# Gated attention and feed-forward kernel: fourth weight block split before the second up product, first low part of h before the softmax sums, output banks filled before the exponential

## The chip, the cores and the metric

The kernel runs on one core of one Trainium2 chip. A core has a matrix engine (TensorE, PE in the profile; PEld is its loading of weights), a vector engine (VectorE, DVE), an activation engine (ScalarE, ACT), a general engine (GpSimd, POOL) and an engine that here only issues transfers (SyncE, SP). ACT and POOL can issue transfers too; ACTq, SPq and POOLq are these issues. Each engine runs its own instructions in program order and waits on semaphores for the others. The metric is device time of one launch in microseconds (us); smaller is better.

## The reference

Everything is float32: 2048 tokens of width 512, 32 heads of 16, a window of 8 keys at distance 2, and a feed-forward part of width 1792 = 14 blocks of 128.

```python
xn  = layernorm(x)
qkv = xn @ wqkv                                    # q, k, v
logits[s, w] = q[s] . k[s - 2 w] / 4               # w = 0 .. 7, per head, masked where s - 2 w < 0
o   = softmax(logits) applied to v[s - 2 w]
s   = o @ wo
h   = relu(xn @ w1 + b1) ** 2
g   = silu(h @ w2 + b2)
out = x + s * g
```

## The kernel before

**Parts.** A float32 matrix product is made from two parts of each operand: a high part (ACT copies the value to the format that PE multiplies at full rate, `high`, line 119) and a low part (value minus high part, on DVE or POOL, `low`, line 122). Three products give the result: high times high, high times low, low times high (`PASSES`, line 25). `split` (line 125) makes both parts of one 128x512 tile. So before PE can use a block of weights, ACT and then POOL must have worked on it.

**Stages.** First come layer norm and the q, k, v products of the 16 token tiles; the last tiles save work with the scheme of `seven` (line 571), whose tiles are named X, Y, Z and U. Then come the four chunks `c` of 512 tokens (loop at line 895) with the feed-forward part. Attention itself runs on DVE beside all of it, as a stream of steps (`attention`, line 239): `qk` makes logits (tiles pr, L), `soft_a` subtracts the maximum (mx) and has ACT take the exponential, `soft_b` (line 288) makes the sums and their reciprocals (sm) on DVE and lets POOL scale L by them, `av` weighs the values (tiles pv, v), and `store_o` writes them out.

**Order by hand.** Every instruction keeps its program order on its engine. How many steps of the attention stream are put between two matrix products is decided by `pump(margin)` (line 366): it keeps an account of PE's and of DVE's time and emits steps while DVE's account stays below PE's plus the margin, in ns (`LATE` is 3000).

**Feed-forward blocks.** `up(c, f)` (line 672) makes block `f` of h for chunk `c`: 12 matmuls into a bank `ph`, then three instructions on ACT: Relu with bias in place, Square to the high part of `h`, Square in place (or into a tile `sq` for some blocks). `lowh(f)` (line 693) makes the low part of `h` on DVE (on POOL for the blocks with `sq`). The banks `ph` of two blocks alternate, so block f + 2 needs block f's bank read by `lowh(f)`. `down(pb, c, f, j)` (line 830) is three matmuls that add block `f`'s share of the output tile `j` to the bank `pb[j]`; PE makes `up(c, f)` and then the four `down` of block f - 2.

**Weight blocks.** The split weights of all 14 blocks stay in the core: `next_w` (line 391) splits the next block `f` (tiles named w: w1r, the block of w1, and w2r, the block of w2) and, from block 3 on, asks for the raw numbers of block f + 2 with `load_w` (line 382). The raw tiles are `piece`s of four buffers (line 116): block 5's raw numbers take the buffers of block 3's, and so can be asked for only when POOL has made block 3's low parts. Blocks 0 to 2 are split within the last stages of q, k, v; block 3 at the end of `seven` (line 661), block 4 ahead of `up(0, 2)`, and so on, one ahead of each `up` of chunk 0.

**The end of `seven`**, lines 653 to 663, for the last tiles: `next_w()` for block 2, `up(0, 0)`, the last product of Z, `pump(LATE)`, `up(0, 1)`, `next_w()` for block 3, `lowh(0)`, `pump(LATE)`.

**Turn from a chunk to the next**, lines 954 to 970: the last `down`, then `gate` for the four output tiles (in chunk 0 DVE adds b2 into tiles z, since the banks did not start from it; then ACT applies Silu to them), then `up(c + 1, 0)` and `up(c + 1, 1)` with a `pump` and `lowh` behind each, then the out product `pw` of an attention tile. The loop's next round starts with the four banks `pb`: from chunk 1 on ACT copies b2 into them (lines 896 to 899) and the matmuls of `down` add to that.

Of the kernel before, what the change touches and what calls it, by code (L numbers as in the profile page):

```python
# [26 lines left out]
TPC = C // P  # L27
# [30 lines left out]
def body(ctx: ExitStack, tc: tile.TileContext, x, wqkv, wo, w1, b1, w2, b2, out):  # L58
# [307 lines left out]
    def pump(margin=-SLACK):  # L366

        limit = clock["PE"] + margin
        flush(clock["PE"])
        while True:  # L370
            if coming[0] is None:
                coming[0] = next(stream, None)
            if coming[0] is None or clock["V"] + coming[0] > limit:
                break
            coming[0] = next(stream, None)
        if coming[0] is None:
            not_before(limit)
# [13 lines left out]
    def next_w():  # L391

        f = len(w12)
        if f < NF:
            w12[f] = buffer(f"w{f}", HOME[f]) if f in HOME else p2.tile([P, 2, 2, 512], FR, name=f"w{f}")
            for i, r in enumerate(raws.pop(f)):
                split(w12[f][:, 0, i], w12[f][:, 1, i], r, G)
            if 2 < f < NF - 2:
                load_w(f + 2)
# [171 lines left out]
    def seven(a):  # L571

        b = a + 1
        for s in (2, 0, 1):
            stgs[s] = pstg.tile([P, 4, 2, P], F32, name=f"stg{a}_{s}", tag="stg", bufs=5)
        sq_, sk_ = stgs[0], stgs[1]

        def x(t, h):
            return lambda p, k: xt[t][:, p, 2 * h + k]

        def s(i):
            return lambda p, k: ss[a][i // 2][:, i % 2, p, k]

        def product(ps, left, w, start=False, stop=False):
            n = 0
            for k in range(2):
                for p, r in PASSES:
                    PE.matmul(ps, left(p, k), w[:, r, k], start=start and n == 0, stop=stop and n == 5,
                              skip_group_check=True)
                    n += 1  # L590

        def groups(ps):
            return ps.rearrange("p (g c) -> p g c", g=4)

        more = a + 2 < NT
        X = psA(f"X{a}")
        product(X, x(a, 0), wq[0], start=True)
        Y = psH(f"Y{a}")
        A.activation(Y, X, AF.Copy)
        if a == SEVEN[0]:  # L600
            sum_high(a)
        first_norm(a)
        second_norm(a)
        pump(LATE)
        qkv(a, 2)
        if a > SEVEN[0]:
            sum_high(a)
        pump(LATE)
        while tail:
            tail.pop()()  # L610
        sum_low(a)
        if more:
            trans(a + 2)
        else:
            load_w(3)
        pump(LATE)
        qkv(b, 2)
        if more:
            trans(b + 2, True)
            lowx(a + 2)  # L620
        pump(LATE)
        product(X, x(a, 1), wq[1], stop=True)
        A.activation(sq_[:, :, 0], groups(X), AF.Copy, scale=0.25)
        pump(LATE)
        product(Y, s(1), tw[T2])
        Z = psH(f"Z{a}")
        A.activation(Z, Y, AF.Copy)
        if more:
            highx(b + 2)
        else:  # L630
            next_w()
        U = psA(f"U{a}")
        product(U, s(0), tw[T1], start=True, stop=True)
        A.activation(sk_[:, :, 0], groups(U), AF.Copy)
        if more:
            lowx(b + 2)
            sum_x(a + 2)
            next_stats(a)
        pump(LATE)
        product(Z, s(2), tw[T3])  # L640
        product(Y, s(3), wq[3], stop=True)
        pump(1500)
        V.tensor_add(sk_[:, :, 1], groups(Z), sk_[:, :, 0])
        V.tensor_add(sk_[:, :, 0], groups(Y), sk_[:, :, 0])
        store(a, 1, sk_)

        def last():
            product(Z, x(b, 1), tw[T4], stop=True)
            A.activation(sq_[:, :, 1], groups(Z), AF.Copy, scale=0.25)
            store(a, 0, sq_)  # L650

        tail.append(last)
        if not more:
            next_w()
            load_w(4)
            pump(LATE)
            up(0, 0, psT)
            tail.pop()()
            pump(LATE)
            up(0, 1, psT)  # L660
            next_w()
            lowh(0)
            pump(LATE)

# [227 lines left out]
    b2t = p2.tile([P, D], F32, name="b2t")  # L892
    dma(b2t, b2[None, :].to_broadcast([P, D]))

    for c in range(NCH):
        last = c == NCH - 1
        pb = [psA(f"pb{c}_{j}") for j in range(TPC)]
        if c:
            for j in range(TPC):
                A.activation(pb[j], b2t, AF.Copy)  # L900
        t0 = c * TPC
        room = ROOM if c else ROOM0
        for f in range(2, NF):
            if c == 0:
                next_w()
            up(c, f)
            pump()
            if c == 0 and f == 3:

                rwo = [p2.tile([P, 2, D], F32, name=f"rwo{i}", tag="oT", bufs=2) for i in range(2)]  # L910
                for i in range(2):
                    for q in range(4):
                        rows = wo[q * P + 64 * i:q * P + 64 * i + 64, :].rearrange("(g p) n -> p g n", g=2)
                        dma(rwo[i][32 * q:32 * q + 32], rows)
            if c == 0:
                if 6 <= f < 10:
                    split(wot[:, 0, f - 6], wot[:, 1, f - 6], rwo[(f - 6) // 2][:, (f - 6) % 2], G)
            elif f == 2:
                finish(t0 - 4)
            elif f == 3:  # L920
                finish(t0 - 3)
                trans_o(t0 - 2, psT(f"pT{t0 - 2}"))
                trans_o(t0 - 1, psT(f"pT{t0 - 1}"))
            elif f == 4:
                lowo(t0 - 2)
                lowo(t0 - 1)
            elif f == 5:
                out_product(t0 - 2, psT(f"pw{t0 - 2}"))
            elif f == 6:
                finish(t0 - 2)  # L930
                out_product(t0 - 1, psT(f"pw{t0 - 1}"))
            elif f == 7:
                finish(t0 - 1)
            if f == 2 and c:
                load_o(c * 2 - 1, True)
            elif f >= 7:
                load_o(c * 2, f >= 9)
            if f == 10:
                for i in range(2):
                    trans_o(t0 + i, psT(f"pT{t0 + i}"))  # L940
            if f == 11:
                for i in range(2):
                    lowo(t0 + i)
            if f >= 12:
                load_o(c * 2 + 1, last and f > 12)
            if not (last and f == NF - 1):
                for j in range(TPC):
                    down(pb, c, f - 2, j)
            pump(room)
            lowh(f)  # L950
        out_product(t0, psT(f"pw{t0}"))
        if last:
            out_product(t0 + 1, psT(f"pw{t0 + 1}"))
        pump(room)
        if not last:
            for i in range(2):
                for j in range(TPC):
                    down(pb, c, NF - 2 + i, j)
                if i == 0:
                    pump(room)  # L960
            pump()
            not_before(clock["PE"])
            for j in range(TPC):
                gate(c, j, pb)
            for i in range(2):
                up(c + 1, i)
                pump(ROOM)
                lowh(i)
            out_product(t0 + 1, psT(f"pw{t0 + 1}"))
            pump(ROOM)  # L970
        else:
            for i in range(2, TPC):
                trans_o(t0 + i, psH(f"pT{t0 + i}"))
            for i in range(2, TPC):
                lowo(t0 + i)
            xl = xTa.tile([P, TPC, 512], F32, name="xlast", tag="xT")
            dma(xl.rearrange("p (h e) n -> p h (e n)", e=2),
                x[t0 * P:(t0 + TPC) * P, :].rearrange("(h p e) n -> p h (e n)", p=P, e=2))
            for j in range(TPC):
                for f in range(NF - 3, NF):  # L980
                    down(pb, c, f, j)
                gate(c, j, pb)
                if j < 2:
                    finish(t0 + j, xl[:, j])
            for j in range(2, TPC):
                n = D // 2 if j == TPC - 1 else D
                for i in range(0, D, n):
                    cols = slice(i, i + n)
                    out_product(t0 + j, (psT if i else psH)(f"pw{t0 + j}_{i}"), cols)
                    finish(t0 + j, xl[:, j], cols)  # L990
# [21 lines left out]
```

## Time and profile before

| | us |
|---|---|
| median of 3 runs | 491.64 |
| these runs | 490.69 to 491.73 |
| the profiled execution, its own time | 489.87 |
| its span, first to last instruction | 487.9 |

The profile is of one execution. Its span leaves out 1.97 us that lie around the first and last instruction. All instructions that go through the helper that keeps the program order bear line 87, so rows are told apart by their tiles. A row of a timeline gives the start in the span, the length, the engine, the operation, what it writes and what it reads, how many it merges, and in brackets how long the engine sat idle before it and who released it. Matmuls overlap: a start-to-start distance of 2.72 us for 12 of them is what the timeline shows wherever nothing waits, while the row of 12 says 2.88 us, because the last of them is still draining. So PE's losses are read from distances between starts.

### The profile page before, as it was taken

What the parts mean: (1) busy time and instruction counts of PE and PEld (TensorE: products, weight loads), DVE (VectorE), ACT (ScalarE), POOL (GpSimd) and SP (SyncE); (2) the same over time, 40 slices, a digit from 0 to 9 for tenths busy, and PEclk for the clock granted to TensorE, in tenths of its full rate; (3) what the DMA queues carried; (4) which work ended last, traced back from release to release, by engine and by line L of the source; (5) the groups of instructions that cost most, each with busy time, mean ns of one, the idle gap of its engine ahead of it and who ended that gap; (6) DMA issues with size and microseconds to landing.
All of it is one profiled execution on the core that took longest, in us unless ns stands there. A gap on an engine that the chain in (4) does not pass through costs nothing.

```text
span 487.9 us, 5921 instructions
## 1 busy us (share of the span) xinstructions
PE 480.0 (98%) x2118; PEld 394.6 (81%) x2118; DVE 438.0 (90%) x374; ACT 227.8 (47%) x403; POOL 173.3 (36%) x153
## 2 busy tenths in 40 slices
PE   8999999999989999999999999999999999999996
PEld 6888888888768888887888888888888888888885
DVE  5997999999996999999999999999999979999243
ACT  5675667635455566327412434552242365223240
POOL 1325343655788998201233130412032014021100
PEclk9999999999999999999999999999999999999999
DMA  8799799994969682815362428255522745150231
GB/s 303 219 297 322 232 293 285 312 354 165 329 217 294 168 269 88 273 60 185 107 184 65 161 79 299 75 174 140 152 74 89 267 132 174 31 152 0 87 103 69
DMA packets 48520, 88.78 MB, mean 182 GB/s; under 512 B 5372, under 2 KB 32364, under 8 KB 45676
## 3 DMA queue, kind: packets, MB, share of 16 engines
q1 hardware_dynamic: 42444, 51.72, 33.9%
q10 hardware_dynamic: 4320, 33.56, 19.4%
q0 software_dynamic: 1728, 3.15, 3.9%
q8 instruction: 16, 0.26, 0.2%
q14 instruction: 12, 0.10, 0.1%
HBM read 57.94 MB, written 27.32 MB: 175 GB/s over the span
## 4 chain that ended last, share of the span: by engine, by line
PE 78%; DVE 9%; issue 6%; POOL 4%; ACT 2%; DMA 1%; ACTq 0%; DVEq 0%; POOLq 0%
PE pb L87 25%; PE ph L87 23%; PE pq L87 13%; PE pw L87 8%; PE X L87 3%; DVE L L87 3%; PE Z L87 3%; PE Y L87 3%; POOL w L87 2%; DVE v L87 2%; PE U L87 1%; DVE h L87 1%; DVE pr L87 1%; POOL ss L87 1%; DVE pv L87 1%
## 5 line engine op out<-in xcount | busy, mean ns | idle before, releaser
L87 PE MATMUL pb<-w,h 128*128 128x512 f32 x672 | 161.1, 389 | 1.2 <-ACT pb L87 0.8
L87 PEld LDWEIGHTS pb<-w,h 128*128 128x128 f32 x672 | 126.0, 188 | 28.2 <-ACT pb L87 1.2
L87 PE MATMUL ph<-xU,w 128*128 128x512 f32 x504 | 120.6, 389 | 0.0
L87 PEld LDWEIGHTS ph<-xU,w 128*128 128x128 f32 x504 | 94.6, 188 | 19.6
L87 ACT ACTIVATE ph<-ph,b1t 128x512 f32<-128x512 f32 x56 | 37.0, 660 | 150.6 <-PE ph L87 141.2
L87 DVE TENSOR_TENSOR pv<-v,L 128x2048 f32<-128x2048 f32 x32 | 78.4, 2449 | 1.3 <-POOL L L87 0.7
L87 DVE TENSOR_TENSOR pr<-k,q 128x2048 f32<-128x2048 f32 x32 | 75.8, 2368 | 0.5
L87 DVE TENSOR_REDUCE L<-pr 128x128 f32<-128x2048 f32 x32 | 73.0, 2280 | 0.4
L87 DVE TENSOR_REDUCE v<-pv 128x256 f32<-128x2048 f32 x32 | 72.7, 2273 | 0.4
L87 POOL TENSOR_TENSOR h<-sq,h 128x512 fp32r<-128x512 f32 x15 | 25.0, 1669 | 84.2 <-ACT sq L87 81.8
L87 DVE TENSOR_TENSOR h<-ph,h 128x512 fp32r<-128x512 f32 x41 | 27.8, 680 | 21.6 <-ACT ph L87 21.6
L87 PE MATMUL pw<-wot,oT 128*128 128x512 f32 (+1 forms) x204 | 46.0, 377 | 0.0
L87 PEld LDWEIGHTS pw<-wot,oT 128*128 128x128 f32 x204 | 36.8, 188 | 7.1
L87 PE MATMUL ph<-xT,w 128*128 128x512 f32 x168 | 40.5, 390 | 0.9 <-POOL w L87 0.9
L87 PEld LDWEIGHTS ph<-xT,w 128*128 128x128 f32 x168 | 31.5, 188 | 7.8 <-POOL w L87 1.3
L87 ACT ACTIVATE h<-ph 128x512 fp32r<-128x512 f32 x56 | 33.5, 599 | 2.6
L87 PE MATMUL pq<-wq,xt 128*128 128x512 f32 x144 | 34.4, 389 | 0.0
L87 POOL TENSOR_TENSOR L<-L,mx_None 128x512 f32<-128x512 f32 x7 | 17.6, 2515 | 41.6 <-DVE mx_None L87 41.6
L87 PEld LDWEIGHTS pq<-wq,xt 128*128 128x128 f32 x144 | 27.0, 188 | 5.6
L87 PE MATMUL pq<-wq,xT 128*128 128x512 f32 x132 | 30.8, 392 | 0.0
L87 PEld LDWEIGHTS pq<-wq,xT 128*128 128x128 f32 x132 | 24.5, 188 | 5.8 <-ACT xT L87 0.7
L87 POOL TENSOR_TENSOR L<-L,sm_None 128x512 f32<-128x512 f32 x7 | 11.4, 1622 | 47.3 <-DVE sm_None L87 47.3
(103 smaller groups left out, 552.7 us busy)
## 6 DMA issues: line engine op xcount, KB each, us to landing
k<-sk ACTq DMA_DIRECT2D x8, 1408.0 KB, 6.4
v<-sv ACTq DMA_DIRECT2D x8, 1408.0 KB, 9.0
sx<-xt SPq DMA_DIRECT2D x12, 512.0 KB, 4.9
xU<-sx ACTq DMA_DIRECT2D x6, 1024.0 KB, 8.9
x<-in_A_x SPq DMA_DIRECT2D x16, 256.0 KB, 5.7
sk<-stg SPq DMA_DIRECT2D x8, 512.0 KB, 4.4
sq<-stg SPq DMA_DIRECT2D x8, 512.0 KB, 4.6
sv<-stg SPq DMA_DIRECT2D x8, 512.0 KB, 5.7
```

The lines of the kernel that those rows point to most:

```text
L87: return tc.keep_in_program_order(f(*a, **k))
```

## The change

Three edits. First, `next_w()` for block 3 is called ahead of `up(0, 1)` and no longer behind it. Second, the `pump` in front of `up(0, 1)` has the margin 1500 in place of 3000, so that fewer steps of attention go ahead of `lowh(0)`. Third, the copies of b2 into the four banks of the next chunk are emitted right behind `up(c + 1, 1)`, ahead of the `pump` there, by a function that remembers the banks.

```diff
@@ -656,9 +656,9 @@
             pump(LATE)
             up(0, 0, psT)
             tail.pop()()
-            pump(LATE)
+            next_w()
+            pump(1500)
             up(0, 1, psT)
-            next_w()
             lowh(0)
             pump(LATE)
 
@@ -892,12 +892,19 @@
+    pbs = {}
+
+    def banks(c):
+        if c not in pbs:
+            pbs[c] = [psA(f"pb{c}_{j}") for j in range(TPC)]
+            if c:
+                for j in range(TPC):
+                    A.activation(pbs[c][j], b2t, AF.Copy)
+        return pbs[c]
+
     for c in range(NCH):
         last = c == NCH - 1
-        pb = [psA(f"pb{c}_{j}") for j in range(TPC)]
-        if c:
-            for j in range(TPC):
-                A.activation(pb[j], b2t, AF.Copy)
+        pb = banks(c)
         t0 = c * TPC
@@ -964,6 +971,8 @@
             for i in range(2):
                 up(c + 1, i)
+                if i == 1:
+                    banks(c + 1)
                 pump(ROOM)
                 lowh(i)
```

The program keeps every instruction it had. In the rows below the number behind a name is that of the buffer: w_1400 is block 2, w_1460 in the kernel before and w_1434 in the changed one are block 3, w_1485 is block 4, and a row that is there in both but under another number shows with - and +.

On POOL, at the start of chunk 0, the rows are the low parts of blocks 2, 3 and 4 and the scaling of L by its sums:

```order
 L87 TENSOR_TENSOR w_1400<-w1r_1155,w_1400 128x512
 L87 TENSOR_TENSOR w_1400<-w2r_1156,w_1400 128x512
+L87 TENSOR_TENSOR w_1434<-w1r_1326,w_1434 128x512
+L87 TENSOR_TENSOR w_1434<-w2r_1327,w_1434 128x512
 L87 TENSOR_TENSOR L_1106<-L_1106,sm_None 128x512
-L87 TENSOR_TENSOR w_1460<-w1r_1326,w_1460 128x512
-L87 TENSOR_TENSOR w_1460<-w2r_1327,w_1460 128x512
 L87 TENSOR_TENSOR w_1485<-w1r_1405,w_1485 128x512
 L87 TENSOR_TENSOR w_1485<-w2r_1406,w_1485 128x512
```

Block 3's two low parts now stand ahead of the scaling, which waits for DVE's reciprocal. On ACT, block 3's two high parts move likewise from behind the three instructions of `ph_1` to ahead of them.

On DVE, at the same place, the rows are the end of an `av` step, the low part of h for block 0, and the sums with their reciprocals:

```order
+L87 TENSOR_REDUCE v_499<-pv_3_1443 128x256
+L87 TENSOR_TENSOR h_0_1422<-ph_0_1409,h_0_1422 128x512
 L87 TENSOR_REDUCE sm_None<-L_1106 128x64
 L87 RECIPROCAL sm_None<-sm_None 128x64
-L87 TENSOR_TENSOR h_0_1422<-ph_0_1409,h_0_1422 128x512
```

The low part of block 0 moved from behind the sums to ahead of them; the row of v stands there in both kernels.

On ACT, at the turn from chunk 0 to chunk 1, the rows are the last instruction of `ph_1`, the four copies of b2, and the exponential of an attention unit (L_1901) with the load of the activation table for it:

```order
 L87 ACTIVATE sq_1_2114<-ph_1_2098 128x512
+L87 ACTIVATE pb_0_2116<-b2t 128x512
+L87 ACTIVATE pb_1_2117<-b2t 128x512
+L87 ACTIVATE pb_2_2118<-b2t 128x512
+L87 ACTIVATE pb_3_2119<-b2t 128x512
 L87 ACT_TABLE_LOAD
 L87 ACTIVATE L_1901<-L_1901 128x512
-L87 ACTIVATE pb_0_2134<-b2t 128x512
-L87 ACTIVATE pb_1_2135<-b2t 128x512
-L87 ACTIVATE pb_2_2136<-b2t 128x512
-L87 ACTIVATE pb_3_2137<-b2t 128x512
```

The copies moved ahead of the load and the exponential. At the two later turns they stood right behind `ph_1` already, and nothing moves there. Two small things move besides: about 25 us into chunk 0 one exponential and one split of `wo` trade places on ACT, and on SP one load of `wo` goes ahead of block 7's loads. PE's order is the same from beginning to end.

## The prediction

> **What bounds the kernel now.** The first page and the table of windows come first. A row of windows gives the stretch, its length, and the busy time and instructions of PE, PEld, DVE, ACT and POOL, then the granted clock, the transfers' share and their rate.
>
> ```profile
> span 487.9 us, 5921 instructions
> PE 480.0 (98%) x2118; PEld 394.6 (81%) x2118; DVE 438.0 (90%) x374; ACT 227.8 (47%) x403; POOL 173.3 (36%) x153
> ...
> 140.00:148.00 8.00, 6.70 (x28) 4.86 (x27) 7.93 (x8) 3.48 (x7) 6.99 (x5) 1.00 0.83 280
> 148.00:211.00 63.00, 63.00 (x280) 52.18 (x279) 58.93 (x39) 34.49 (x59) 46.33 (x25) 1.00 0.69 213
> 211.00:225.00 14.00, 13.21 (x59) 10.58 (x57) 13.73 (x11) 8.25 (x14) 2.38 (x2) 1.00 0.32 117
> 225.00:300.00 75.00, 74.98 (x331) 62.11 (x332) 73.74 (x52) 27.06 (x46) 19.03 (x11) 1.00 0.45 141
> ```
>
> PE is the bound: busy for 480.0 of 487.9 us at full clock (1.00), and what the kernel can win without less arithmetic is PE's idle time. Two of these stretches hold it: 140 to 148, the start of chunk 0, and the end of 211 to 225, the turn to chunk 1. Between them and behind them PE is busy throughout. The timeline of PE shows the places:
>
> ```profile
> 140.48 0.61 PE L87 MATMUL pb<-w,h 128*128 128x512 f32 x2
> 141.53 2.60 PE L87 MATMUL pb<-w,h 128*128 128x512 f32 x10 [0.43 <-DVE h L87]
> 143.97 0.62 PE L87 MATMUL ph<-xT,w 128*128 128x512 f32 x2
> 145.46 2.56 PE L87 MATMUL ph<-xT,w 128*128 128x512 f32 x10 [0.87 <-POOL w L87]
> 147.86 2.88 PE L87 MATMUL pb<-w,h 128*128 128x512 f32 x12
> ...
> 221.30 2.91 PE L87 MATMUL ph<-xU,w 128*128 128x512 f32 x12
> 225.02 3.01 PE L87 MATMUL pb<-w,h 128*128 128x512 f32 x12 [0.81 <-ACT pb L87]
> 227.87 2.88 PE L87 MATMUL ph<-xU,w 128*128 128x512 f32 x12
> ```
>
> The reader sees three waits: the low part of h for block 0 (DVE), the low part of weight block 3 (POOL), and the copy of b2 into the bank (ACT). They are the three edits' targets. The bracketed idle understates them, so I go by starts. From 140.48 to 147.86 PE makes 24 matmuls in 7.38 us; at 2.72 us for 12 these take 5.44, so the first two waits cost **1.94 us**. From 221.30 to 227.87 it makes 24 in 6.57 us, so the third costs **1.13 us**. All else that PE loses (the first 7 us, the drain at the end, some 0.1 to 0.2 us at the last products of Z) lies outside the change. The most that these edits can give directly is 1.94 + 1.13 = 3.07 us.
>
> **Edits one and two, the start of chunk 0.** The rows of POOL, ACT, DVE and SP at this place:
>
> ```profile
> 135.24 3.33 POOL L87 TENSOR_TENSOR w<-w2r,w 128x512 fp32r<-128x512 f32 x1
> 141.01 1.08 POOL L87 TENSOR_TENSOR L<-L,sm_None 128x512 f32<-128x512 f32 x1 [2.44 <-DVE sm_None L87]
> 142.05 3.35 POOL L87 TENSOR_TENSOR w<-w1r,w 128x512 fp32r<-128x512 f32 x1
> 145.36 1.29 POOL L87 TENSOR_TENSOR w<-w2r,w 128x512 fp32r<-128x512 f32 x1
> ...
> 137.96 0.66 ACT L87 ACTIVATE ph<-ph,b1t 128x512 f32<-128x512 f32 x1 [2.11 <-PE ph L87]
> 139.67 0.62 ACT L87 ACTIVATE w<-w1r 128x512 fp32r<-128x512 f32 x1
> 150.71 0.63 ACT L87 ACTIVATE w<-w1r 128x512 fp32r<-128x512 f32 x1 [7.20 <-DMA w1r<-in_B_w]
> 151.91 0.64 ACT L87 ACTIVATE ph<-ph,b1t 128x512 f32<-128x512 f32 x1
> ...
> 137.46 2.29 DVE L87 TENSOR_REDUCE v<-pv 128x256 f32<-128x2048 f32 x1
> 139.67 0.68 DVE L87 TENSOR_REDUCE sm_None<-L 128x64 f32<-128x512 f32 x1
> 140.85 1.22 DVE L87 TENSOR_TENSOR h<-ph,h 128x512 fp32r<-128x512 f32 x2
> 141.99 2.28 DVE L87 TENSOR_TENSOR pr<-k,q 128x2048 f32<-128x2048 f32 x1
> 153.70 0.69 DVE L87 TENSOR_TENSOR h<-ph,h 128x512 fp32r<-128x512 f32 x1 [3.66 <-ACT ph L87]
> ...
> 139.78 0.53 SPq L319 DMA_DIRECT2D so<-v  x1
> 140.40 0.54 SPq L549 DMA_DIRECT2D sq<-stg  x1
> 145.43 0.37 SPq L387 DMA_DIRECT2D w1r<-in_B_w  x1
> ```
>
> - *Low part of h, block 0.* It runs at 139.67 in the sums' place and is done by 139.67 + 0.68 = 140.35. PE needs it at its third matmul, 140.48 + 2 x 0.227 = 140.93. Covered by 0.6 us. The sums end 0.6 us later; only POOL's scaling waits for them.
> - *High parts of block 3 on ACT.* Two copies of at most 0.62 us each go from 139.67 into the 2.11 us in which ACT waited for PE ahead of 137.96. That idle time hides them; without it `ph_1` would be 1.24 us late. ACT waited for no transfer at 139.67, so the raw numbers are there.
> - *Low parts of block 3 on POOL.* POOL is free at 135.24 + 3.33 = 138.57, and was idle until 141.01 for the reciprocal. They now run from 138.57: one by 139.87, both by 141.15, at 1.29 us each (the row at 145.36). PE needs the first at 140.48 + 2.72 + 0.45 = 143.65. Covered by 3.8 us, even at the 3.35 us that such an operation takes beside DVE's large products (142.05).
> - *What follows on POOL.* The scaling starts at about 141.6 instead of 141.01, next to DVE's product at 141.99. Its cost there is between its 1.08 us and the 3.35 us of the row at 142.05. Then block 4's first low part, 1.29 to 3.35 us. With the long value for both it is done at 141.6 + 6.7 = 148.3; PE needs it in its next up product, at 148.64 + 0.45 = 149.1. I take the long value for the scaling and the short one for block 4: 146.3, nothing waits.
> - *Block 5's load.* Its transfer on SP stood at 145.43 because it waited for the low part of block 3 (ends 145.40). Now that wait ends at 139.87 and the order on SP decides: it follows the store of q, 140.40 + 0.54, so it is issued at about 141.0, 4.4 us earlier.
>
> ```profile
> DMA to landing us min/median/max: 2.9/4.9/5.6
> ```
>
> This is the answer on w1r's tile: from issue to landing at most 5.6 us. So the first half of block 5 is there by 146.6, the second by about 147.1. ACT then makes its two high parts and the three instructions of `ph_3` by about 149.5 instead of 153.67 (151.91 + 1.76). DVE, which waited 3.66 us for these, is ready at 150.04. So **DVE wins its 3.66 us**, with 0.5 us to spare on ACT's side; no PE wait hangs on it at this point, but the turn does.
>
> A rule of the Trainium skill speaks against this step: "DMA: Bandwidth & Descriptors", section "Queues, rings and completion order", says that each engine of the transfers goes round between the queues that have work, so the load of v (1408 KB on ACT's queue, issued at 142.94) would share the rate with block 5's. The load measured here shared with it as well, so the landing row already holds that; by the rule the spare half microsecond could go, not the 3.07.
>
> **Edit three, the turn.** The rows of DVE and ACT before PE's third wait:
>
> ```profile
> 215.50 2.48 DVE L87 TENSOR_TENSOR z<-pb,b2t 128x512 f32<-128x512 f32 x4
> ...
> 222.55 1.28 ACT L87 ACT_TABLE_LOAD   x1
> 224.38 2.14 ACT L87 ACTIVATE pb<-b2t 128x512 f32<-128x512 f32 x4
> ```
>
> ACT is a chain here: Silu behind DVE's additions, two blocks of h, the table load, the exponential, then the copies. PE started 225.02 - 224.38 = 0.64 us after the first copy did. With the copies ahead of the load the first starts at 222.55, 1.83 us earlier, and PE may start at 223.19. It would be there at 221.30 + 2.72 = 224.02, so on that clock the wait is gone with 0.8 us to spare, and the other three copies (2.14 / 4 = 0.54 us each) keep ahead of PE's three matmuls for a bank (0.68 us). But PE now comes 1.94 us earlier, at 222.08, and the copy comes earlier only by what DVE won, since ACT's chain hangs on the additions. With 3.66 us won, the additions start at about 211.84 (PE ended the banks three products ahead of 221.30, at 213.14, now 211.2), and the copies at 222.55 - 3.66 = 218.9, some 3 us before PE. DVE needs to win only 223.19 - 222.08 = 1.11 us for the wait to go whole.
>
> Given back: the exponential now comes behind 2.14 us of copies, but its reader, the sums, stands behind four `av` steps of DVE. The three instructions of `ph_2` behind it keep their place, since the same work precedes them. At the later turns nothing moves and PE waits for nothing. Behind 227.87 PE runs without a gap to the end in the kernel before, with DVE busy 73.74 of 75 us; DVE is moved up at least as far as PE (3.66 against 3.07 us), so no wait should form.
>
> **Sum.** 1.94 + 1.13 = 3.07 us. The profiled execution would take 489.87 - 3.07 = 486.8 us (span 484.8). Its time is 1.77 us below the median of the runs; carried to the median, 491.64 - 3.07 = **488.6 us**, 0.62% less.
>
> **Rivals.**
>
> *DVE becomes the bound of the turn.* If block 5's load lands no earlier than before, or the scaling stretches DVE's product and the wait at 153.70 stays, the additions still start at 215.50. Then PE may start on the banks at 223.19 and wins 225.02 - 223.19 = 1.83 us in all, whatever it won at 140: 489.8 us. For it: DVE has next to no idle time from 153.70 to 218. Against it: the load goes 4.4 us earlier, and a move of 1.11 us is enough.
>
> *The edits miss.* If the first low part stays late because the reduce at 137.46 moves, PE loses 141.53 - 140.93 = 0.60 us there again and the sum is 2.47, 489.2 us. If both new orders are taken up by waits right behind them (block 4 a microsecond or two late, then the turn on DVE's clock), the gain falls below 1 us: about 491 us, no change that can be told.
>
> *Slower: POOL held by DVE.* Block 4's low part now stands behind a scaling that begins just as DVE starts a large product. From 148.3 (two held operations) PE's need at 149.1 is 0.8 us away; each further held operation costs 3.35 us. It decides against the change once block 4 is done after 149.1 + 3.07 = 152.2. With two further holds it is done at 155.0, PE waits 5.9 us and loses 2.8 on balance: 494.5 us. For it: two of the three low parts of w in the rows above took over 3.3 us. Against it: never more than one operation was held per DVE product, and there is one product in this stretch.
>
> The Trainium skill's "GPSIMD Engine Reference", section "Specifications", says that GpSimd shares its SBUF interfaces with VectorE and contends with instructions that have two SBUF inputs. The trace agrees: 3.35 us beside the product of k and q at 141.99, 1.29 us at 145.36. By the rule block 3's low parts, now beside a reduce, stay short, and only the scaling is exposed, which is how it was priced above.
>
> **Chances and range.** The forecast 0.68; DVE at the turn or the first wait left (489.2 to 489.8) 0.17; no change that can be told 0.10; slower 0.05. The range reaches down to where runs scatter (the fastest run of before lies 0.95 below the median, the profiled one 1.77: 488.6 less 1.4 is 487.2) and up past the DVE rival with the same scatter of some 0.4 us, 490.2. About 0.2%, 1 us, is what a measurement here can tell from no change; the cases faster by more than that are the first two, 0.85; within it 0.10; slower 0.05.
>
> **What would show it.** Right: PE's starts from the pb row of block 0 on stand 2.72 us apart without a bracket; ACT's wait for w1r of block 5 shrinks from 7.20 us and ends by 147; DVE's 3.66 us before the low part of h is gone; the additions z start about 212; the first copy stands ahead of the table load, and PE's bracket with ACT pb is gone. Wrong: a bracket on PE naming POOL w one block later, DVE's wait for ACT ph still there, or new brackets on PE behind the turn, where there are none now.

## The result and the profile after

The changed kernel takes 488.07 us (median of 6 runs, 486.48 to 488.28) against 490.63 us for the kernel before, timed beside it (6 runs, 489.64 to 491.73). The ratio of the means, 487.70 to 490.75 us, is **0.9938**, with a 95% interval of 0.9917 to 0.9959: 3.04 us or 0.62% less. The forecast was 3.07 us, 0.62%. The medians lie only 2.56 us (0.52%) apart and the interval reaches from 0.41 to 0.83%, so it is luck that the two percentages agree to the digit. The forecast time of 488.6 us started from a median of 491.64 us for the kernel before, which beside the changed one stands at 490.63.

First come the page's head and the same windows as before (PE, PEld, DVE, ACT, POOL, clock, transfers' share and rate), of the changed kernel:

```profile
span 485.0 us, 5918 instructions
PE 478.9 (99%) x2118; PEld 394.4 (81%) x2118; DVE 439.8 (91%) x374; ACT 228.2 (47%) x403; POOL 173.7 (36%) x153
...
140.00:148.00 8.00, 8.00 (x37) 6.62 (x36) 7.93 (x8) 4.18 (x9) 7.49 (x5) 1.00 0.92 316
148.00:211.00 63.00, 63.00 (x279) 52.09 (x278) 62.55 (x40) 32.52 (x56) 43.69 (x24) 1.00 0.69 208
211.00:225.00 14.00, 13.96 (x63) 11.22 (x61) 13.76 (x12) 10.20 (x17) 2.38 (x2) 1.00 0.38 142
```

PE has no idle time left in the first stretch (6.70 of 8.00 us busy before) and next to none in the third (13.21 of 14.00 before). The span is 2.9 us shorter. In the second stretch it is DVE that changed: busy for 62.55 us where it was 58.93. The timeline of PE in the changed kernel, at the two places:

```profile
140.31 2.88 PE L87 MATMUL pb<-w,h 128*128 128x512 f32 x12
143.03 2.88 PE L87 MATMUL ph<-xT,w 128*128 128x512 f32 x12
145.75 2.88 PE L87 MATMUL pb<-w,h 128*128 128x512 f32 x12
...
216.51 2.88 PE L87 MATMUL pw<-wot,oT 128*128 128x512 f32 x12
219.43 3.02 PE L87 MATMUL ph<-xU,w 128*128 128x512 f32 x12
222.28 2.88 PE L87 MATMUL pb<-w,h 128*128 128x512 f32 x12
```

At the start of chunk 0 the 24 matmuls take 145.75 - 140.31 = 5.44 us: all 1.94 us are won. At the turn no bracket names ACT's copies any more, but two distances are still long: 219.43 - 216.51 = 2.92 and 222.28 - 219.43 = 2.85, where 2.72 is the rule. Together PE loses 0.33 us there, and of the 1.13 us 0.80 are won: 2.74 in all in this profile. (The span is shorter by 0.17 us more, because PE was that much earlier at the first row of pb.) The table of waits for the weight loads of PE between 210 and 230 us says what the remainder is (who waited, for whom, us in total, times, longest):

```profile
PEld ph L87 <- DVE h L87: 0.5, 1, 0.5
```

The third up product of chunk 1 needs the bank of the first, and that one is read by DVE's low part of h. In the kernel before this row of DVE was:

```profile
220.34 0.69 DVE L87 TENSOR_TENSOR h<-ph,h 128x512 fp32r<-128x512 f32 x1 [0.17 <-ACT ph L87]
```

It ended at 221.03, and PE began the third up product 0.27 us later, at 221.30. In the changed kernel it ends at 219.37 (row of 218.68 below), and PE begins 0.06 us later. So about 0.21 us were spare before, and since PE comes 1.94 us earlier to this point, DVE must win about 1.73 us if PE is not to wait here. The other engines at the start of chunk 0, in the changed kernel:

```profile
138.34 1.29 POOL L87 TENSOR_TENSOR w<-w1r,w 128x512 fp32r<-128x512 f32 x1
141.40 1.09 POOL L87 TENSOR_TENSOR L<-L,sm_None 128x512 f32<-128x512 f32 x1 [0.51 <-DVE sm_None L87]
142.45 3.34 POOL L87 TENSOR_TENSOR w<-w1r,w 128x512 fp32r<-128x512 f32 x1
153.21 1.29 POOL L87 TENSOR_TENSOR w<-w1r,w 128x512 fp32r<-128x512 f32 x1 [1.62 <-ACT w L87]
159.27 1.29 POOL L87 TENSOR_TENSOR w<-w2r,w 128x512 fp32r<-128x512 f32 x1
...
139.46 0.68 DVE L87 TENSOR_TENSOR h<-ph,h 128x512 fp32r<-128x512 f32 x1
141.78 2.85 DVE L87 TENSOR_TENSOR pr<-k,q 128x2048 f32<-128x2048 f32 x1
147.47 2.97 DVE L87 TENSOR_TENSOR pr<-k,q 128x2048 f32<-128x2048 f32 x1
153.27 3.37 DVE L87 TENSOR_TENSOR pr<-k,q 128x2048 f32<-128x2048 f32 x1
159.47 3.25 DVE L87 TENSOR_TENSOR pr<-k,q 128x2048 f32<-128x2048 f32 x1
213.84 2.48 DVE L87 TENSOR_TENSOR z<-pb,b2t 128x512 f32<-128x512 f32 x4
218.68 0.69 DVE L87 TENSOR_TENSOR h<-ph,h 128x512 fp32r<-128x512 f32 x1 [0.17 <-ACT ph L87]
...
146.04 0.63 ACT L87 ACTIVATE w<-w1r 128x512 fp32r<-128x512 f32 x1 [3.74 <-DMA w1r<-in_B_w]
152.50 0.63 ACT L87 ACTIVATE w<-w1r 128x512 fp32r<-128x512 f32 x1 [3.50 <-DMA w1r<-in_B_w]
220.46 2.17 ACT L87 ACTIVATE pb<-b2t 128x512 f32<-128x512 f32 x4
...
140.83 0.84 SPq L387 DMA_DIRECT2D w1r<-in_B_w  x1
145.81 0.38 SPq L387 DMA_DIRECT2D w1r<-in_B_w  x1
```

Block 3's low parts run from 138.34, the first low part of h at 139.46, block 5's load goes at 140.83 and is there at 146.04: each step within some 0.6 us of where the prediction put it. DVE's wait of 3.66 us is gone. But its additions z start at 213.84, not at 211.84. Set against the first row of pb, which the two profiles have at 140.48 and 140.31, they come 1.49 us earlier. DVE won less than half of what was forecast, and the question for the experiments was where the rest went and whether it matters.

### The profile page after: what moved, and what is told of

Read it like the earlier page. It is cut to its first block, busy times and chain, and to the rows that moved or that the text cites. A ratio compares the mean times of both kernels' runs of the same rounds, so it can differ in the third digit from the quotient of the medians.

```text
span 485.0 us, 5918 instructions
## 1 busy us (share of the span) xinstructions
PE 478.9 (99%) x2118; PEld 394.4 (81%) x2118; DVE 439.8 (91%) x374; ACT 228.2 (47%) x403; POOL 173.7 (36%) x153
## 4 chain that ended last, share of the span: by engine, by line
PE 98%; DMA 1%; DVE 0%; POOL 0%; issue 0%; ACT 0%; POOLq 0%
PE ph L87 31%; PE pb L87 31%; PE pq L87 14%; PE pw L87 9%; PE Z L87 3%; PE Y L87 3%; PE X L87 3%; PE U L87 2%; DMA x<-in_A_x 1%; PE pxT L87 0%; DVE z L87 0%; DVE st L87 0%; POOL rs L87 0%; DVE xn L87 0%; ACT scratch L87 0%
## 5 line engine op out<-in xcount | busy, mean ns | idle before, releaser
L87 DVE TENSOR_TENSOR pr<-k,q 128x2048 f32<-128x2048 f32 x32 | 78.3, 2447 | 0.6
```

The lines of the kernel that those rows point to most:

```text
L87: return tc.keep_in_program_order(f(*a, **k))
```

## The experiments

PE's loss below is the sum of its distances over 2.72 us for 12 matmuls, from the first row of pb on. DVE's gain is the start of the additions z minus the start of that row, against the kernel before (215.50 - 140.48 = 75.02 us).

| kernel | PE loses at the start | at the turn | elsewhere | DVE's gain | ratio of times, interval |
|---|---|---|---|---|---|
| before | 1.94 | 1.13 | 0 | 0 | 1 |
| changed, 1st profile | 0 | 0.33 | 0 | 1.49 | 0.9938, 0.9917 to 0.9959 |
| changed, 2nd | 0 | 0 | 0 | 2.47 | 0.9935, 0.9913 to 0.9958 |
| changed, 3rd | 0 | 0.34 | 0.09 | 1.45 | |
| edit one | 0.78 | 0 | 0 | 2.54 | 0.9959, 0.9945 to 0.9973 |
| edit two | 0 | 1.14 | 0 | 1.94 | 0.9972, 0.9957 to 0.9986 |
| edits one and two | 0 | 0.48 | 0 | 2.30 | 0.9945, 0.9933 to 0.9957 |
| edit three | 1.92 | 0.02 | 0 | -0.01 | 0.9981, 0.9970 to 0.9992 |
| low parts left out | 0 | 0 | 0 | 3.36 | |
| Silu later | 0 | 0.04 | 0.23 | 1.53 | 0.9940, 0.9918 to 0.9961 |
| more loads | 0 | 0.36 | 0.53 | 0.98 | |
| POOL held | 0 | 0.35 | 0.87 | 0.66 | |

The theory to test was the prediction's: three separate waits, and behind them DVE, which needs to win 1.11 us so that the turn does not take back what the start gave. Its rivals: DVE sets the turn, the waits hang on one edit, POOL becomes the bound.

**Edit one alone.**

```diff
             tail.pop()()
+            next_w()
             pump(LATE)
             up(0, 1, psT)
-            next_w()
             lowh(0)
```

> Edit one alone: block 3 is split ahead of the second up product, the margin stays 3000, the copies of b2 stay where they were. The low part of h for block 0 then stays behind the sums, so the theory of separate waits expects PE's wait on DVE h to stay (24 matmuls from the first pb row in 5.44 + 0.6 = 6.0 us, before 7.38) and its wait on POOL w to go: 1.3 us won at the start of chunk 0. At the turn the first copy still stands behind the table load and the exponential, and comes earlier only by what DVE wins (1.5 us by the changed kernel's trace): in all 1.3 to 1.5 us. If both waits hang on the one edit, all 1.94 us are won at the start.

PE's timeline of this kernel:

```profile
140.43 0.61 PE L87 MATMUL pb<-w,h 128*128 128x512 f32 x2
141.49 2.60 PE L87 MATMUL pb<-w,h 128*128 128x512 f32 x10 [0.44 <-DVE h L87]
143.92 2.89 PE L87 MATMUL ph<-xT,w 128*128 128x512 f32 x12
146.65 2.88 PE L87 MATMUL pb<-w,h 128*128 128x512 f32 x12
```

The wait on block 3 goes, the wait on the low part of h stays: 146.65 - 140.43 - 5.44 = 0.78 us. So the two waits are separate. The turn, though, lost nothing, without edit three: PE came 0.78 us later and DVE had won 2.54 us, more than expected, and the copies stood ready behind the exponential. In all 2.29 us, where 1.3 to 1.5 were expected.

**Edit two alone.**

```diff
             tail.pop()()
-            pump(LATE)
+            pump(1500)
             up(0, 1, psT)
             next_w()
```

> Edit two alone: the margin is 1500, block 3 is split behind the second up product as before. On DVE the low part of h goes ahead of the sums, and on POOL the scaling of L falls behind block 3's low parts too, since the step of attention is emitted later. ACT makes block 3's high parts at about 139.7 to 140.7, so POOL could make the first low part by about 141.6, ahead of PE's need at 143.6. If edit two carries the start by itself: 24 matmuls from the first pb row in 5.44 us, 1.94 us won, and edit one is worth only the earlier load of block 5 (issued at about 141.7 instead of 140.83). If edit one is needed for block 3: PE's wait on POOL w stays, and 0.6 us are won there.

POOL and PE of this kernel:

```profile
140.10 1.29 POOL L87 TENSOR_TENSOR w<-w1r,w 128x512 fp32r<-128x512 f32 x1 [1.80 <-ACT w L87]
...
140.22 2.88 PE L87 MATMUL pb<-w,h 128*128 128x512 f32 x12
142.94 2.88 PE L87 MATMUL ph<-xT,w 128*128 128x512 f32 x12
145.66 2.88 PE L87 MATMUL pb<-w,h 128*128 128x512 f32 x12
219.11 2.92 PE L87 MATMUL ph<-xU,w 128*128 128x512 f32 x12
222.83 3.02 PE L87 MATMUL pb<-w,h 128*128 128x512 f32 x12 [0.80 <-ACT pb L87]
```

Both waits at the start go by this edit alone. It puts the sums behind the low part of h on DVE, and with them POOL's scaling behind block 3; block 3's first low part waits for ACT until 140.10 and is still 2 us early. At the turn the old wait stands unchanged (1.14 us): PE comes 1.94 us earlier and DVE wins 1.94, so the copies move exactly as far as PE does. This is the mechanism of the rival in which DVE sets the turn: the copies hang on DVE's additions.

**Edits one and two, without three.** The two edits above together.

> Edits one and two, without three. As the prediction had it (DVE wins 3.66 us) the copies would be early enough behind the exponential too, and edit three worth nothing: 3.07 us won. By the changed kernel's trace, where DVE won 1.5 us, the first copy would start at 220.46 + 1.28 + 0.53 = 222.3 and PE on the banks 0.64 later, at 222.9, against 222.28 with edit three: PE's wait on ACT pb is back with 0.6 to 0.9 us, and about 2 us are won in all.

PE and DVE of this kernel:

```profile
219.37 2.88 PE L87 MATMUL ph<-xU,w 128*128 128x512 f32 x12
222.44 3.01 PE L87 MATMUL pb<-w,h 128*128 128x512 f32 x12 [0.19 <-ACT pb L87]
225.29 2.88 PE L87 MATMUL ph<-xU,w 128*128 128x512 f32 x12
...
156.88 0.69 DVE L87 TENSOR_TENSOR h<-ph,h 128x512 fp32r<-128x512 f32 x1 [1.12 <-ACT ph L87]
```

PE wins 2.59 us and waits for the copies again, 0.48 us with the restart. So without edit three 0.48 us are left at the turn, where a gain of 3.66 us on DVE would have left nothing; with edit two alone 1.14 are left, and with edit one alone, where PE comes later, nothing. What edit three has to win hangs on how far DVE gets ahead of PE. (Edit three beside only one of the others was not run.) PE wins a little more here than DVE's 2.30 us, because ACT also had 0.44 us of idle time ahead of its second block of h in the kernel before and has 0.15 now. By the times alone this kernel cannot be told from the changed one.

**Edit three alone.** The function `banks` and its call behind `up(c + 1, 1)`, with the old order at the end of `seven`.

> Edit three alone. The start of chunk 0 stays as in the kernel before (7.38 us for the 24 matmuls, both waits there). At the turn the copies stand ahead of the table load, 1.83 us earlier on ACT; PE is there 1.0 us earlier than now, so its wait on ACT pb goes whole: 1.1 us won. If the wait only changes its name (the bank of the next up product, the exponential's reader), less than 0.5 us is won.

PE's timeline at the turn:

```profile
221.79 2.90 PE L87 MATMUL ph<-xU,w 128*128 128x512 f32 x12
224.53 2.88 PE L87 MATMUL pb<-w,h 128*128 128x512 f32 x12
```

The start is as before (1.92 us lost), the turn loses 0.02 us: 1.11 us won, as expected. The wait on the copies changed to no other name.

**The changed kernel again**, beside two variants of it.

> The changed kernel again, beside the next two on the same chip: ratio 0.994, PE's starts as in its first profile (24 matmuls from the first pb row in 5.44 us; 0.2 us late at the third up product of chunk 1, whose bank waits for the low part of h of its first block).

Here PE's distances are 2.72 us throughout; the turn loses nothing and the whole 3.07 us are won. The third profile, below, lost 0.34 there. What differs is DVE. Its timeline in this second profile, with one row of POOL:

```profile
153.27 3.34 DVE L87 TENSOR_TENSOR pr<-k,q 128x2048 f32<-128x2048 f32 x1
159.44 2.29 DVE L87 TENSOR_TENSOR pr<-k,q 128x2048 f32<-128x2048 f32 x1
159.68 3.20 POOL L87 TENSOR_TENSOR w<-w2r,w 128x512 fp32r<-128x512 f32 x1 [0.31 <-ACT w L87]
212.82 2.47 DVE L87 TENSOR_TENSOR z<-pb,b2t 128x512 f32<-128x512 f32 x4
```

The product at 159.44 takes 2.29 us where the first profile had 3.25, and z starts 1.02 us earlier (212.82 against 213.84). POOL's row says why. In the first profile POOL's operation began at 159.27, 0.20 us ahead of the product, ended at 160.56, and the product ended 2.16 us behind that. In the second it began at 159.68, 0.24 us behind the product; the product kept its 2.29 us, and POOL's row grew to 3.20. So the one that starts first runs its length, and the other ends nearly as if it had begun when the first was done.

All profiles here bear this out (the one with POOL held is left aside, since its rows are merged). Of their 155 products of two tiles (pr and pv) between 130 and 215 us, the 62 that found no operation of POOL running took 2.28 to 2.29 us, and the 93 that found one ended 2.14 to 2.18 us behind its end.

> The changed kernel a third time, for its profile: PE's starts at the turn show whether the 0.33 us that the first profile lost there (none in the second) come and go with the start of DVE's additions z (213.84 in the first, 212.82 in the second). Expected: below 213.5 no loss, above it 0.1 to 0.4 us.

DVE in the third profile:

```profile
214.04 2.47 DVE L87 TENSOR_TENSOR z<-pb,b2t 128x512 f32<-128x512 f32 x4
```

Here z starts at 214.04, and the turn loses 0.34 us: the loss comes and goes with DVE, as expected. (Of the times, this run is a single one: 487.32 us.)

**Low parts of blocks 5 to 13 left out.** ACT writes zeros in their place, so POOL's subtraction is gone.

```diff
-                split(w12[f][:, 0, i], w12[f][:, 1, i], r, G)
+                if f < 5:
+                    split(w12[f][:, 0, i], w12[f][:, 1, i], r, G)
+                else:
+                    high(w12[f][:, 0, i], None, r)
+                    A.activation(w12[f][:, 1, i], r, AF.Copy, scale=0.0)
```

> The changed kernel with the low parts of the weight blocks 5 to 13 left out: ACT writes zeros in their place, POOL's subtraction is gone. If POOL's operations stretch DVE's large products (2.29 us alone, up to 3.37 in the changed kernel's rows between 148 and 193), the products fall to about 2.3 us except beside the low parts of wo and the scaling of L, DVE's additions z start 2 to 3 us earlier than 213.84, and PE's 0.2 us at the third up product of chunk 1 go. If ACT or the transfers set DVE's pace, the additions stay at about 213.8.

DVE of this kernel:

```profile
147.78 2.29 DVE L87 TENSOR_TENSOR pr<-k,q 128x2048 f32<-128x2048 f32 x1
153.13 2.29 DVE L87 TENSOR_TENSOR pr<-k,q 128x2048 f32<-128x2048 f32 x1
157.51 0.69 DVE L87 TENSOR_TENSOR h<-ph,h 128x512 fp32r<-128x512 f32 x1 [2.09 <-ACT ph L87]
212.24 2.47 DVE L87 TENSOR_TENSOR z<-pb,b2t 128x512 f32<-128x512 f32 x4
```

Without POOL's operations beside them the second, third and fourth product take 2.29 us each (the first, still beside block 4's low part, takes 2.85 as in the changed kernel), the gain on DVE is 3.36 us, and PE loses nothing. So POOL's operations do stretch them. About 1.5 of the 3.36 us come from four products between 171 and 195, which POOL stretched in the kernel before too, so the figure is not what the change by itself would win without the stretch. And a wait of 2.09 us stands behind the third product: DVE waits for ACT, which waits for the load of block 6 (and then, in this kernel, also writes the zeros). That is the second half of the answer: the wait of 3.66 us did not only go, part of it moved one block on.

**Silu behind the first up block of chunk 1**, meant to take the last 0.33 us.

```diff
-        A.activation(z, pb[j] if c else z, AF.Silu)
+        else:
+            A.activation(z, pb[j], AF.Silu)
...
                 up(c + 1, i)
+                if c == 0 and i == 0:
+                    for j in range(TPC):
+                        A.activation(gs[c, j], gs[c, j], AF.Silu)
```

> The changed kernel with chunk 0's four Silu moved behind ACT's three instructions of chunk 1's first up block. If the 0.33 us that PE still loses at the turn come from the low part of h waiting for ACT behind the Silu, DVE makes it without its 0.17 us of idle time, PE's distance of 2.92 us ahead of the third up product falls to 2.72 to 2.8, and the kernel wins 0.2 to 0.3 us more on PE's starts (too little for the times). If the late Silu holds ACT's next block, the copies of b2 come late instead and PE waits for ACT pb again, 0.3 us or more lost.

DVE's 0.17 us of idle time goes and the third up product starts on time (0.04 us lost at the turn), with DVE as late as in the first profile (1.53). But PE then loses 0.23 us two up products on, where its weight load waits for DVE's low part of h again. The loss moved; this is no better kernel.

**More loads ahead of block 6's.**

```diff
     dma(b2t, b2[None, :].to_broadcast([P, D]))
+    for n in range(2):
+        dma(p2.tile([P, D], F32, name=f"more{n}", tag=f"sq", bufs=2), w2[n * P:(n + 1) * P, :])
```

> The changed kernel with two further loads of 256 KB, which nothing reads, ahead of block 6's on SP. If DVE's gain is cut by block 6's load (ACT waited 3.5 us for it and DVE up to 2.1 us behind ACT), it lands some 1.5 us later than 152.5 (512 KB at the 340 GB/s of this stretch), DVE's wait behind the third product grows to 2 to 4 us, and the additions z start 1 to 2 us later than in the changed kernel, at 214 to 215; PE then loses at the turn (ph behind DVE h or pb behind ACT) 0.3 to 1.5 us. If products stretched by POOL are all that cuts it, z stays at 212.8 to 213.8 and PE as it was.

Block 6 is there at 153.38, 13.3 us behind the first row of pb, against 12.2 in the first and second profile of the changed kernel and 13.2 in the third: not clearly later, so the 512 KB did not do what they were meant to. DVE's gain is 0.98 us, less than in any of the three (1.45 to 2.47), z starts at 214.11, and PE loses 0.89 us in all, always for DVE's low part of h. But DVE's wait behind the third product is 1.36 us, not the 2 to 4 expected and no longer than the 1.52 of the third profile; the rest is in the five large products, which take 13.76 us: 3.66 - 1.27 - 1.36 = 1.03 of the measured 0.98. So this is no test of the load.

**POOL held.** Block 4's first low part is made three times.

```diff
                 split(w12[f][:, 0, i], w12[f][:, 1, i], r, G)
+                if f == 4 and i == 0:
+                    for n in range(2):
+                        low(w12[f][:, 0, i], w12[f][:, 1, i], r, G)
```

> The changed kernel with the first low part of block 4 made three times over on POOL (the same values). It ends at 145.8 now, and PE needs it at 149.1 by the prediction's sum. Two more operations of 1.3 to 3.3 us end it at 148.4 to 152.4; one of them falls beside DVE's product at 147.5, so about 150.4: PE waits about 1.3 us for POOL w in the up product of block 4, and the 24 matmuls from the pb row of block 1 take 6.7 instead of 5.44 us. If PE does not wait for POOL here, the slower rival's place was wrong.

POOL and PE of this kernel:

```profile
142.65 6.10 POOL L87 TENSOR_TENSOR w<-w1r,w 128x512 fp32r<-128x512 f32 x3
...
145.92 2.88 PE L87 MATMUL pb<-w,h 128*128 128x512 f32 x12
148.64 2.88 PE L87 MATMUL ph<-xT,w 128*128 128x512 f32 x12
151.36 2.88 PE L87 MATMUL pb<-w,h 128*128 128x512 f32 x12
```

The three take 6.10 us and end at 148.75, 0.3 us before PE needs the value; only one of them was held. PE waits for nothing there. It loses 0.87 us between 176 and 190 and 0.35 at the turn instead, for DVE's low parts of h. The place of the slower rival was wrong: in this one profile POOL's delay reaches PE through DVE.

## Why the prediction was right, and what in it was not

- **The two waits at the start, 1.94 us: right.** All profiles with both edits show 5.44 us. The edits overlap, which the prediction did not see: edit two alone is enough for PE, since it moves POOL's scaling too.
- **The wait at the turn, 1.13 us: right as a wait, a little short as a gain.** No profile of the changed kernel waits for the copies. They start at 220.46, 1.8 us before PE. What is won there is 1.13 us in one profile and 0.8 in the two others. The sum of 3.07 us is reached in the second profile (span 484.6, forecast 484.8); the others stand at 2.74 and 2.64.
- **DVE wins 3.66 us: wrong in size.** It won 1.45 to 2.47. The working took the wait away and kept the length of what stood behind it. In the first profile the five large products from 141.78 to 166.21 take 2.85 + 2.97 + 3.37 + 3.25 + 2.35 = 14.79 us; before they took 2.28 + 2.94 + 2.36 + 2.29 + 2.62 = 12.49. 3.66 - 2.30 = 1.36 of the measured 1.49. With edits one and two they take 12.74, and a wait of 1.12 stands at 156.88: 3.66 - 0.25 - 1.12 = 2.29 of the measured 2.30. The second profile (13.77, no wait) gives 2.38 of 2.47, the third (13.16, a wait of 1.52) 1.47 of 1.45. So the accounts close: products stretched by POOL, and a wait for block 6. Block 6's load goes at 145.81 and is there at 152.50, 6.7 us, where the prediction counted with 5.6 at most for block 5 and never asked for the next.
- **"No wait should form" behind the turn: wrong in two of three profiles,** by 0.33 us. The step that failed is the sentence that DVE, moved up 3.66 against PE's 3.07, is further ahead than before. The third up product waits for the bank of the first unless DVE wins about 1.73 us, as the rows of the kernel before already show: the first and third profile lose 0.33 and 0.34 at 1.49 and 1.45, nothing is lost at 1.94 (edit two alone) and above. The condition named, 1.11 us on DVE for the copies, was right for the copies and not the tightest.
- **The rival in which DVE sets the turn** has a real mechanism: with edit two alone the copies, and PE behind them, move by the 1.94 us that DVE won. Its condition, that DVE wins nothing, did not come about, and in the changed kernel edit three takes the copies off PE's path.
- **POOL beside DVE.** The scaling was to take the long time and block 4's low part the short one; it was the other way round (1.09 and 3.34). The scaling, at 141.40, began before DVE's product at 141.78 and so made the product wait (2.85 us), and block 4's low part, at 142.45, then waited for the product. Block 4's first low part was done at 145.79, forecast 146.3. The Trainium skill's rule on the shared interfaces ("GPSIMD Engine Reference", section "Specifications") agrees with the kernel without low parts, where the products that POOL left alone fall to 2.29 us. It was used for one side only; the cost that counted lay on DVE's products.

The load of block 6 also could not come 3.66 us earlier. It waits until POOL is done with block 4's first raw tile, and went at 147.92 in the kernel before, so the 145.81 of the changed one is 2.1 us earlier:

```profile
147.92 0.84 SPq L387 DMA_DIRECT2D w1r<-in_B_w  x1
```

When block 6's weights come decides between the stretched third product and the wait at 157. Where ACT starts on them 12.2 us behind the first row of pb or earlier (first and second profile, edit two alone), POOL's low part gets ahead of the product (153.21 against 153.27 in the first profile) and stretches it, and DVE does not wait. Where it starts 12.3 to 13.3 us behind (third profile, edit one, edits one and two, Silu later, more loads), the product takes 2.29 us and DVE then waits 1.12 to 1.59. What stays open is why the load takes 6.7 us; the run with more loads did not delay it enough to say.

## What to carry to other kernels

A wait on the engine that bounds is worth its distance between starts, restart included, not its bracket; added up that way, three waits forecast the gain within a few tenths of a us. When a wait goes, ask of the engine that gets ahead what it meets next: here the next load in the chain and the other engine's operations took back 1.2 to 2.2 of DVE's 3.66 us. And look for the tightest reader: the copies needed 1.11 us from DVE, the bank of the next up product 1.73. Of the wait that a reordering on a third engine is meant for, nothing, half or all may be left once the other two have moved; try the edits apart before keeping all of them.

## What the runs showed of the hardware that was not expected

DVE's product of two tiles in the core's memory and POOL's operations take turns: whichever starts first runs its length, and the other is done only 2.14 to 2.18 us (a product) or 1.13 to 1.17 us (a low part) behind the first one's end. So the product takes 2.29 us alone and up to 3.37 behind a subtraction of POOL, and POOL's 1.29 us become up to 3.37 behind a product. A few tenths of a us decide which of them is first, and that differs between runs of one program. Together with the time at which block 6 comes it moved DVE by up to 1.2 us (z at 212.82, 213.84, 214.04) and PE by 0.3 to 0.4 us.
